# Second MoE under a fixed order of all engines, with an order, banks and places of its own for the first quad

## The chip, the cores and the metric

One core of one Trainium2 chip runs one program: attention, a first MoE and a second MoE, one after the other. The metric is the device time of one execution in microseconds. Engines are named as in the profile: PE (TensorE), DVE (VectorE), ACT (ScalarE), POOL (GpSimd), SP (SyncE, which here only starts DMAs).

## The reference, cut to what matters

The change lies in the last stage. Its input `x` is what attention and the first MoE give, 2304 tokens of 512 values. All of it is computed in float32 (weights arrive as 64-bit floats and are decoded on the chip).

```python
def _moe2_ref(x, w_in, w_out):      # w_in 512 x 2048, w_out 2048 x 512
    h = np.maximum(x @ w_in, 0.0)
    return (h * h @ w_out).astype(np.float32)
```

## The kernel before, in words

The program has two phases. Phase 1 (attention and the first MoE) is written out as a list of tokens, `CFG["phase1"]`, and runs under a manual order of all engines (line 916). Its last products are four `yp` banks; `y_out` (line 614) copies each from PSUM to `ys` on ACT (line 617) and writes it to DRAM with a DMA that ACT starts (line 618).

Phase 2, the second MoE, starts at line 920. There only PE has a manual order: DVE, ACT, POOL and SP are put in order by a list scheduler that works with modelled times, ahead of the run.

**Tiles and quads.** The 2304 tokens are three tiles `t` of 768 (`T2`), and the 2048 columns of `w_in` are eight quads `q` of 256. A tile and a quad make two 2x2 block matrices, multiplied by Strassen's scheme in Winograd's form: seven products P1, P6, P2, P7, P5, P4, P3, in that order (`PRODUCTS`, line 704), each six matmuls of 128x384, since every float32 operand is split into a high and a low half (`mm3`, line 188: high by high, high by low, low by high). The tile's seven operands (A11, A12, A22 and the sums S1 to S4) come from rows `yr` that are read from DRAM (`y_sums`, line 868; sums at line 889), and are split by `y_part` (ACT makes the high half `h...` at line 908, DVE or POOL the low half `l...` at line 910).

**Banks.** `quad` (line 973) has two PSUM banks for the seven products, x and y, which change places from quad to quad. P1 and P2 add up in the first, then P5 and P3 in it; P6, P7 and P4 take turns in the second. So P2 waits for the copy `p` of P1 (ACT, line 994), P7 for u2 (DVE, line 997), P5 for c11 (ACT, line 1000), P4 for u3 (DVE, line 1005), P3 for c22 (DVE, line 1008). The six other banks, `po` (o0 to o5), hold the tile's output and are free in its first quad until `out_group` (line 942) starts them.

**After the products.** Four results c11, c22, c21, c12 are squared (line 1001 for c11, line 982 for the others) and split by `split_g` (ACT `gh`, line 938; DVE `gl`, line 939). From them come twelve output groups of three 128x512 matmuls, two for each of the six `po` banks; they stand between the products of the next quad (line 1018). After a tile's last quad the `po` banks are copied to `ob` (two buffers; the even ones by ACT, line 955, the odd ones by DVE, line 953) and written out by SP (line 957).

**Weights.** Quads 0 to 2 are decoded in phase 1. Quad 3 is decoded by `decode_quad` (line 744), which belongs to phase 2: raw words are loaded (line 167), put together on DVE (lines 172, 181, 184, 739 to 742) and ACT (line 178), and split by `split_cut` (line 727; ACT high half, line 730, POOL low half, line 731). Quads 4 to 7, and all quads of the later tiles, are loaded again from copies in DRAM (`load_quad`, line 858, DMAs at line 864). `spread` (line 1027) puts such steps behind given products.

Of the kernel before, what the change touches and what calls it, by code (L numbers as in the profile page):

```python
# [18 lines left out]
P = 128  # L19
# [98 lines left out]
def local_global_attention__then__moe_kernel(  # L118
# [589 lines left out]
    EARLY = ("A11", "S2", "A12")  # L708
    w2_t = {}
# [34 lines left out]
    def decode_quad(q):  # L744

        raw, tb = {}, {}

        def begin(key, src):
            low, high = raw[key] = raw_words(src, f"{key}_{q}")
            rebias(high)  # L750
            low_bits(low, low)

        def end(key):
            low, high = raw[key]
            join(low, high, low)
# [16 lines left out]
        def last(c, key):  # L772
            end(key)
            split_cut(q, c, raw[key])

        f = 2 * q
        return [
            lambda: begin("f0", wi2[f]),
            lambda: begin("f1", wi2[f + 1]),
            both,  # L780
            other,
            lambda: sums(raw, tb),
            lambda: (split_cut(q, "i1", tb["f0"]), begin("o0", wo2[f]), keep("i0", "i3")),
            lambda: (split_cut(q, "i2", tb["f1"]), begin("o1", wo2[f + 1]), keep("i1", "i2")),
            lambda: last("o0", "o0"),
            lambda: (last("o1", "o1"), keep("o0", "o1")),
        ]
# [132 lines left out]
    with tc.manual_schedule(engines={ENG.PE}):  # L920
# [6 lines left out]

        def product(t, q, ps, a, c, c0, first):
# [6 lines left out]
        def split_g(t, q, name, c):  # L935
            ghi = gp.tile([P, TH], F32R, tag="gh", name=f"gh{t}{q}{name}", bufs=6)
            glo = gp.tile([P, TH], F32R, tag="gl", name=f"gl{t}{q}{name}", bufs=6)
            nc.scalar.activation(out=ghi, in_=c, func=AF.Copy)  # L938
            nc.vector.tensor_tensor(out=glo, in0=c, in1=ghi.bitcast(F32), op=ALU.subtract)  # L939
            return ghi, glo  # L940

        def out_group(t, k, q, i, f, g, last):
# [7 lines left out]
            if last:  # L950
                o = gp.tile([P, DM], F32, tag="ob", name=f"ob{t}_{i}", bufs=2)
                if i % 2:
# [3 lines left out]
                r0 = t * T2 + i * P  # L956
                nc.sync.dma_start(out=out[r0 : r0 + P, :], in_=o)

        def out_groups(t, k, q, g):
# [3 lines left out]
            if k == NQ - 1:  # L963
                order = [(n, i) for i in (0, 1, 2) for n in ("11", "12")] + [(n, i) for i in (3, 4, 5) for n in ("22", "21")]
# [8 lines left out]
        def quad(t, k, q, outs, after):  # L973

            f = lambda tag, name, bufs: gp.tile([P, TH], F32, tag=tag, name=f"{name}{t}{q}", bufs=bufs)
            bank = "xy" if (t * NQ + k) % 2 == 0 else "yx"
            new = lambda j, n: ps_i.tile([P, 512], F32, tag=bank[j], name=f"{n}_{t}{q}")
# [3 lines left out]
            def square(name, c):  # L981
                V.scalar_tensor_tensor(out=c, in0=c, scalar=0.0, in1=c, op0=ALU.max, op1=ALU.mult)  # L982
                g[name] = split_g(t, q, name, c)

            for j, (p, a, c, c0) in enumerate(PRODUCTS):
                if p in ("P2", "P3"):
                    b = ps["P1" if p == "P2" else "P5"]
                else:
                    b = ps[p] = new(p in ("P6", "P7", "P4"), p)
                product(t, q, b, a, c, c0, p not in ("P2", "P3"))  # L990
                d = b[:, 0:TH]
                if p == "P1":
                    got["p1"] = f("p1", "p", 1)
                    A.activation(out=got["p1"], in_=d, func=AF.Copy)
                elif p == "P6":
                    got["u2"] = f("u2", "u2", 1)
                    V.tensor_tensor(out=got["u2"], in0=d, in1=got["p1"], op=ALU.add)  # L997
                elif p == "P2":
                    e = f("c", "c11", 3)
                    A.activation(out=e, in_=d, func=AF.Relu)  # L1000
                    V.tensor_tensor(out=e, in0=e, in1=e, op=ALU.mult)  # L1001
                    g["11"] = split_g(t, q, "11", e)
                elif p == "P7":
                    got["u3"] = f("u3", "u3", 1)
                    V.tensor_tensor(out=got["u3"], in0=d, in1=got["u2"], op=ALU.add)
                elif p == "P5":
                    e = f("c", "c22", 3)
                    V.tensor_tensor(out=e, in0=d, in1=got["u3"], op=ALU.add)
                    square("22", e)
                elif p == "P4":  # L1010
                    e = f("c", "c21", 3)
                    V.tensor_tensor(out=e, in0=got["u3"], in1=d, op=ALU.subtract)
                    square("21", e)
                else:
                    e = f("c", "c12", 3)
                    V.tensor_tensor(out=e, in0=d, in1=got["u2"], op=ALU.add)
                    square("12", e)
# [15 lines left out]
        spread(0, 0, [lambda a=a: y_split(0, a, nc.vector) for a in ("S1", "A22", "S4")], 0)  # L1033
        turns = [list(range(NQ)), [4, 5, 6, 7, 0, 1, 2, 3], list(range(NQ))]
        spread(0, 0, decode_quad(3))
        for t, k in ((t, k) for t in range(NT2) for k in range(NQ - 4)):
            one, two = load_quad(turns[t][k + 4])
            spread(t, k + 1, [one], 1)
            spread(t, k + 2, [two], 1)
        for t in range(NT2 - 1):  # L1040
            spread(t, 5, y_sums(t + 1), 0, 2)
            for j, (_, a, _, _) in enumerate(PRODUCTS):
                spread(t, NQ - 1, [lambda t=t, a=a, j=j: y_split(t + 1, a, nc.gpsimd if j % 2 else nc.vector)], j)
        outs = []
# [53 lines left out]
```

## Time and profile before

| | us |
|---|---|
| three runs, median (lowest to highest) | 826.97 (826.06 to 827.83) |
| the profiled execution, its own time | 826.54 |
| its span, first to last instruction | 824.7 |
| granted TensorE clock, mean | 0.998 |
| PE busy | 807.5 (98%) |
| DVE busy | 522.3 (63%) |
| ACT busy | 321.6 (39%) |
| POOL busy | 184.8 (22%) |

Phase 2 begins on PE at 434.17 us of the span. An engine's idle time is listed with what ended it. Matmuls overlap: the distance between two starts is what a matmul costs, its own length is longer. A busy PE may still run at half its clock, which the distance between starts shows.

### The profile page before, as it was taken

Reading aid. Unit: us, or ns where it says so; the run is one execution under the profiler, and the core shown is the slowest. Engines: PE = TensorE matmul, PEld = TensorE weight load, DVE = VectorE, ACT = ScalarE, POOL = GpSimd, SP = SyncE. Lnnn points to the kernel's source line nnn. Section 1 sums busy time; section 2 is a strip of 40 time slices with the busy share of each in tenths; the row PEclk is TensorE's granted clock in tenths of the full one; section 3 lists DMA queues with packets and bytes.
Section 4 is the critical chain, followed back from the end, with each engine's and each line's share of the span. In section 5 each row is a group of like instructions: output and inputs, shape, how many; then the busy total and the mean of one; then the engine's idle time right before and its main releaser. Section 6 shows DMA issues by size and latency. Waiting matters only on the chain.

```text
span 824.7 us, 15455 instructions
## 1 busy us (share of the span) xinstructions
PE 807.5 (98%) x6130; PEld 748.7 (91%) x6130; DVE 522.3 (63%) x960; ACT 321.6 (39%) x886; POOL 184.8 (22%) x201
## 2 busy tenths in 40 slices
PE   9899999999999999999998999999999999999997
PEld 8789998999999999999997889988898888898886
DVE  5988998797878854326697554467445456444443
ACT  5776555664556523334444121143112133112111
POOL 4665584342025300202544000020000011000000
PEclk9999999999999999999999999999999999999999
DMA  9835437645479500231897653007454003543102
GB/s 279 233 133 198 160 111 242 193 152 175 142 268 309 171 8 8 77 101 39 286 393 257 233 192 113 1 1 230 156 173 130 27 1 117 190 166 117 50 1 77
DMA packets 60624, 121.84 MB, mean 148 GB/s; under 512 B 5288, under 2 KB 29192, under 8 KB 60552
## 3 DMA queue, kind: packets, MB, share of 16 engines
q1 hardware_dynamic: 55944, 116.13, 42.3%
q10 hardware_dynamic: 4608, 4.72, 1.8%
q8 instruction: 48, 0.79, 0.4%
q14 instruction: 24, 0.20, 0.1%
HBM read 88.33 MB, written 32.51 MB: 147 GB/s over the span
## 4 chain that ended last, share of the span: by engine, by line
PE 85%; DVE 7%; DMA 5%; issue 1%; ACT 1%; SPq 0%; POOL 0%; ACTq 0%; DVEq 0%
PE g L189 9%; PE g L191 9%; PE g L190 9%; PE po L190 8%; PE po L189 8%; PE po L191 8%; PE P L189 7%; PE P L191 7%; PE P L190 7%; PE yp L189 3%; PE yp L191 3%; PE yp L190 3%; DMA raw_p<-in_wg 2%; DMA yr<-y 1%; DMA raw_p<-in_wo 1%
## 5 line engine op out<-in xcount | busy, mean ns | idle before, releaser
L189 PE MATMUL g<-xhi,hi_p 128*128 128x256 f32 (+1 forms) x576 | 174.9, 304 | 0.0
L191 PE MATMUL g<-xhi,lo_p 128*128 128x256 f32 (+1 forms) x576 | 170.3, 296 | 0.9 <-DVE lo_p L562 0.9
L190 PE MATMUL g<-xlo,hi_p 128*128 128x256 f32 (+1 forms) x576 | 169.9, 295 | 0.2 <-DVE xlo L517 0.2
L938 ACT ACTIVATE gh<-c 128x384 fp32r<-128x384 f32 x96 | 50.4, 525 | 182.1 <-DVE c L982 163.7
L189 PEld LDWEIGHTS g<-xhi,hi_p 128*128 128x128 f32 x576 | 108.3, 188 | 1.9
L191 PEld LDWEIGHTS g<-xhi,lo_p 128*128 128x128 f32 x576 | 108.2, 188 | 1.3 <-DVE lo_p L562 1.3
L190 PEld LDWEIGHTS g<-xlo,hi_p 128*128 128x128 f32 x576 | 108.7, 189 | 0.4 <-DVE xlo L517 0.4
L939 DVE TENSOR_TENSOR gl<-c,gh 128x384 fp32r<-128x384 f32 x96 | 56.3, 587 | 48.3 <-ACT gh L938 48.2
L591 DVE TENSOR_TENSOR c<-g,c 128x320 f32<-128x320 f32 (+1 forms) x96 | 43.0, 451 | 38.1 <-PE g L191 30.3
L189 PE MATMUL yp<-hh,hi_p 128*128 128x256 f32 (+1 forms) x192 | 58.6, 305 | 0.0
L191 PE MATMUL yp<-hh,lo_p 128*128 128x256 f32 (+1 forms) x192 | 56.8, 296 | 0.0
L190 PE MATMUL yp<-hl,hi_p 128*128 128x256 f32 (+1 forms) x192 | 56.8, 296 | 0.0
L910 POOL TENSOR_TENSOR lS<-s,hS 128x768 fp32r<-128x768 f32 x2 | 3.7, 1841 | 214.8 <-DVE u L997 116.4
L1001 DVE TENSOR_TENSOR c<-c 128x384 f32<-128x384 f32 x24 | 14.3, 597 | 51.4 <-ACT c L1000 51.4
L598 ACT ACTIVATE hh<-c 128x256 fp32r<-128x256 f32 (+1 forms) x48 | 21.0, 441 | 56.5 <-DVE c L591 56.4
L982 DVE SCALAR_TENSOR_TENSOR c<-c 128x384 f32<-128x384 f32 x72 | 41.3, 574 | 2.3
L1000 ACT ACTIVATE c<-P 128x384 f32<-128x384 f32 x24 | 11.8, 492 | 73.9 <-PE P L191 73.9
L323 POOL TENSOR_TENSOR vd<-v 72x128 f32<-72x128 f32 x32 | 21.0, 656 | 81.1 <-PE o30B L473 52.0
L322 POOL TENSOR_TENSOR v<-v 72x256 f32<-72x256 f32 x32 | 26.5, 827 | 47.5 <-DMA v<-in_vP 47.5
L189 PEld LDWEIGHTS yp<-hh,hi_p 128*128 128x128 f32 x192 | 36.3, 189 | 0.6
L190 PEld LDWEIGHTS yp<-hl,hi_p 128*128 128x128 f32 x192 | 36.4, 190 | 0.0
L191 PEld LDWEIGHTS yp<-hh,lo_p 128*128 128x128 f32 x192 | 36.4, 189 | 0.0
(1351 smaller groups left out, 2112.4 us busy)
## 6 DMA issues: line engine op xcount, KB each, us to landing
raw_p<-in_wg SPq DMA_DIRECT2D x9, 1024.0 KB
raw_f<-in_wi SPq DMA_DIRECT2D x7, 1024.0 KB
raw_o<-in_wo SPq DMA_DIRECT2D x7, 1024.0 KB
k<-in_kT SPq DMA_DIRECT2D x16, 291.0 KB
q<-in_qT SPq DMA_DIRECT2D x16, 288.0 KB
v<-in_vP SPq DMA_DIRECT2D x32, 144.0 KB
out_y<-ob SPq DMA_DIRECT2D x18, 256.0 KB
raw_p<-in_wo SPq DMA_DIRECT2D x3, 1024.0 KB
```

Of the source, the lines that this page charges most:

```text
L189: nc.tensor.matmul(ps, whi, xhi, start=first, stop=False, skip_group_check=more)
L190: nc.tensor.matmul(ps, whi, xlo, start=False, stop=False, skip_group_check=more)
L191: nc.tensor.matmul(ps, wlo, xhi, start=False, stop=last, skip_group_check=more)
L322: nc.gpsimd.tensor_tensor(out=v4[:, c, 0:2], in0=v4[:, c, 0:2], in1=v4[:, c, 2:4], op=ALU.add)
L323: nc.gpsimd.tensor_tensor(out=vd[:, c], in0=v4[:, c, 0], in1=v4[:, c, 1], op=ALU.add)
L591: nc.vector.tensor_tensor(out=c_t[b, h, f], in0=ps[:, 0:N], in1=c_t[b, h, f], op=ALU.max)
L598: nc.scalar.activation(out=hhi, in_=c_t[b, h, f], func=AF.Copy)
L938: nc.scalar.activation(out=ghi, in_=c, func=AF.Copy)
L939: nc.vector.tensor_tensor(out=glo, in0=c, in1=ghi.bitcast(F32), op=ALU.subtract)
L982: V.scalar_tensor_tensor(out=c, in0=c, scalar=0.0, in1=c, op0=ALU.max, op1=ALU.mult)
L1000: A.activation(out=e, in_=d, func=AF.Relu)
L1001: V.tensor_tensor(out=e, in0=e, in1=e, op=ALU.mult)
```

## The change

1. Phase 2 puts all five engines under the order in which the code is written. `AFTER` says what follows each product on ACT and DVE; the last split of a quad (h12, l12) comes "late", behind the next quad's first copy. All low halves of tile operands go to DVE.
2. The first quad of the first tile has its own order, `FIRST_QUAD`, and its products P7, P5 and P4 go to the banks o5, o4 and o3 instead of x and y.
3. Quad 3 is decoded in quads 1 to 3, step by step; its raw words are loaded as a step of their own.
4. Places in SBUF: `ys` of the last half batch gets four buffers in another pool and its DMAs start on SP; the first tiles of each tag of phase 2 are set up ahead (`HOMES`, `kept`).
5. The rows of the next tile are asked for in quad 2 of a tile (counted from 0) instead of quad 5, its sums are formed in quads 5 and 6, its operands split in quad 7 and the first quad of the next tile.
6. The output copies of tiles 0 and 1 are all on ACT. The order of the last quad's output groups changes, and the last `ob` is copied and written in two halves, ACT's first, then DVE's.

```diff
     def y_out(b, h, d):
...
+        if (b, h) == (B - 1, 1):
+            ys = yq.tile([P, 320], F32, tag="ys", name=f"ys{b}{h}{d}", bufs=4)[:, 0:N]
+        else:
+            ys = tmp.tile([P, 320], F32, tag="c", name=f"ys{b}{h}{d}")[:, 0:N]
...
-        nc.scalar.dma_start(out=yscr[b][h][:, d, :], in_=ys)
+        (nc.sync if (b, h) == (B - 1, 1) else nc.scalar).dma_start(out=yscr[b][h][:, d, :], in_=ys)
...
+    FRESH = {"P7": "o5", "P5": "o4", "P4": "o3"}
+    late = []
+    AFTER = {
+        "P1": "copy late", "P6": "u2", "P2": "c11 s11 h11", "P7": "u3 l11", "P5": "c22 s22 h22",
+        "P4": "c21 l22 s21 h21", "P3": "c12 s12 l21",
+    }
+    FIRST_QUAD = """
+        HS3 P1 LS3 copy P6 HS1 u2 P2 LS1 HA22 c11 LA22 P7 HS4 P5 u3 P4 LS4 c22 s11 P3 h11 s22 l11 h22 c21 s21 l22 h21
+    """
...
-    with tc.manual_schedule(engines={ENG.PE}):
+    with tc.manual_schedule(engines={ENG.PE, ENG.DVE, ENG.Activation, ENG.Pool, ENG.SP}):
...
+        HOMES = {"ob": (DM, F32, 2), "gl": (TH, F32R, 6), "gh": (TH, F32R, 6), "c": (TH, F32, 3)}
...
+        quad_tiles(3)
+        for tag in HOMES:
+            kept[tag] = home_of(tag, f"{tag}_first")
...
+                if key == (NT2 - 1, 5):
+                    for n, cols in enumerate((slice(0, 256), slice(256, DM))):
+                        if n:
+                            nc.vector.tensor_copy(o[:, cols], po[key][:, cols])
+                        else:
+                            nc.scalar.activation(out=o[:, cols], in_=po[key][:, cols], func=AF.Copy)
+                        (nc.sync if n else nc.scalar).dma_start(out=out[r0 : r0 + P, cols], in_=o[:, cols])
+                    return
+                if i % 2 and t == NT2 - 1:
                     nc.vector.tensor_copy(o, po[key])
                 else:
                     nc.scalar.activation(out=o, in_=po[key], func=AF.Copy)
...
-                order = [(n, i) for i in (0, 1, 2) for n in ("11", "12")] + [(n, i) for i in (3, 4, 5) for n in ("22", "21")]
+                order = order[:4] + order[9:] + order[4:9]
...
+            def new(n):
+                if (t, k) == (0, 0) and n in FRESH:
+                    return ps_o.tile([P, 512], F32, tag=FRESH[n], name=f"{n}_{t}{q}")
+                return ps_i.tile([P, 512], F32, tag=bank[n in ("P6", "P7", "P4")], name=f"{n}_{t}{q}")
...
+            if (t, k) == (0, 0):
+                for token in FIRST_QUAD.split():
+                    run(token)
+                late.extend(lambda x=x: run(x) for x in ("c12", "s12", "l21", "h12", "l12"))
+                return out_groups(t, k, q, g)
+
+            for j, (p, *_) in enumerate(PRODUCTS):
+                multiply(p)
+                for token in AFTER[p].split():
+                    run(token)
                 for call in outs[len(outs) * j // 7 : len(outs) * (j + 1) // 7]:
                     call()
                 for call in after.get(j, ()):
                     call()
+            late.extend((lambda: hi("c12"), lambda: lo("c12")))
...
-        spread(0, 0, decode_quad(3))
+        steps = decode_quad(3)
+        for n, at in enumerate((0, 2, 4, 6, 7, 8, 9, 11, 14, 16)):
+            spread(0, 1, [steps[n]], at)
...
-            spread(t, 5, y_sums(t + 1), 0, 2)
...
+            load, *rest = y_sums(t + 1)
+            spread(t, 2, [load])
+            spread(t, 5, rest, 2, 2)
+            for (_, a, _, _), at in zip(PRODUCTS, (0, 2, 3, 5, 6, 8, 10)):
+                here, at = ((t, NQ - 1), at) if at < 7 else ((t + 1, 0), at - 7)
+                spread(*here, [lambda t=t, a=a: y_split(t + 1, a, nc.vector)], at)
```

In `FIRST_QUAD` a token is a product (P1), a step of `AFTER`, or H and L with an operand: its high half on ACT, its low half on DVE. s squares, h and l split.

What moves, at three places. ACT, from the first operand split of phase 2 on (hS, hA: high halves of operands; p: copy of P1; w3i, w3o: high halves of quad 3's weights; c: c11). Before:

```order
L908 ACTIVATE hS_0_6056<-yr_5274 128x768
L994 ACTIVATE p_6067<-P_00_6060 128x384
L908 ACTIVATE hS_0_6069<-s_0_5278 128x768
L908 ACTIVATE hA_0_6086<-yr_5274 128x768
L908 ACTIVATE hS_0_6106<-s_0_5280 128x768
L730 ACTIVATE w3i_6110<-raw_f_3_6073 128x512
L730 ACTIVATE w3i_6113<-raw_f_3_6073 128x256
L730 ACTIVATE w3i_6111<-raw_f_3_6073 128x512
L730 ACTIVATE w3i_6112<-raw_f_3_6073 128x512
L730 ACTIVATE w3o_6114<-raw_o_3_6167 128x512
L730 ACTIVATE w3o_6115<-raw_o_3_6167 128x512
L1000 ACTIVATE c_6099<-P_00_6060 128x384
```

With the change:

```order
L924 ACTIVATE hS_0_6069<-yr_5274 128x768
L1029 ACTIVATE p_first<-P_00_6071 128x384
L924 ACTIVATE hS_0_6088<-s_0_5278 128x768
L924 ACTIVATE hA_0_6099<-yr_5274 128x768
L1040 ACTIVATE c_first<-P_00_6071 128x384
L924 ACTIVATE hS_0_6111<-s_0_5280 128x768
L1051 ACTIVATE gh_first<-c_first 128x384
L1051 ACTIVATE gh00c_6142<-c_6130 128x384
```

The six splits of quad 3's weights no longer stand ahead of c11.

DVE in the first quad of tile 1 (u: u2 and u3; s, yr: sums of tile 2's operands at line 889; ob: output copies). Before:

```order
L997 TENSOR_TENSOR u_7135<-P_14_7128,p_7123 128x384
L889 TENSOR_TENSOR s_2_7787<-yr_7783 128x768
L1001 TENSOR_TENSOR c_7152<-c_7152 128x384
L953 COPY ob_1_7162<-po_1_6219 128x512
L889 TENSOR_TENSOR yr_7783<-yr_7783 128x2x384
L889 TENSOR_TENSOR s_2_7788<-s_2_7787,yr_7783 128x768
L939 TENSOR_TENSOR gl_7156<-c_7152,gh_7155 128x384
L1005 TENSOR_TENSOR u_7175<-P_14_7168,u_7135 128x384
```

With the change:

```order
L1033 TENSOR_TENSOR u_7128<-P_14_7121,p_7112 128x384
L926 TENSOR_TENSOR lA_1_7138<-yr_6323,hA_1_7136 128x768
L1045 TENSOR_TENSOR c_7146<-c_7146 128x384
L1033 TENSOR_TENSOR u_7166<-P_14_7159,u_7128 128x384
L1057 TENSOR_TENSOR gl14c_7168<-c_7146,gh14c_7149 128x384
L926 TENSOR_TENSOR lS_1_7178<-s_1_6330,hS_1_7176 128x768
```

Tile 2's sums have left this quad (they now stand in the sixth and seventh quad of tile 1); two low halves of tile 1's operands have come in.

PE's last output groups (the first four of twelve; po2_0 is bank o0 of tile 2). Before:

```order
L189 MATMUL po2_0_8307<-w15o0_8722,gh2711_9090 128x512
L190 MATMUL po2_0_8307<-w15o0_8722,gh2711_9090 128x512
L191 MATMUL po2_0_8307<-w15o0_8722,gl2711_9091 128x512
L189 MATMUL po2_0_8307<-w15o1_8723,gh2712_9161 128x512
L190 MATMUL po2_0_8307<-w15o1_8723,gh2712_9161 128x512
L191 MATMUL po2_0_8307<-w15o1_8723,gl2712_9162 128x512
L189 MATMUL po2_1_8320<-w15o0_8722,gh2711_9090 128x512
L190 MATMUL po2_1_8320<-w15o0_8722,gh2711_9090 128x512
L191 MATMUL po2_1_8320<-w15o0_8722,gl2711_9091 128x512
L189 MATMUL po2_1_8320<-w15o1_8723,gh2712_9161 128x512
L190 MATMUL po2_1_8320<-w15o1_8723,gh2712_9161 128x512
L191 MATMUL po2_1_8320<-w15o1_8723,gl2712_9162 128x512
```

With the change:

```order
L189 MATMUL po2_0_8307<-w15o0_8753,gh27c11_9090 128x512
L190 MATMUL po2_0_8307<-w15o0_8753,gh27c11_9090 128x512
L191 MATMUL po2_0_8307<-w15o0_8753,gl27c11_9107 128x512
L189 MATMUL po2_1_8320<-w15o0_8753,gh27c11_9090 128x512
L190 MATMUL po2_1_8320<-w15o0_8753,gh27c11_9090 128x512
L191 MATMUL po2_1_8320<-w15o0_8753,gl27c11_9107 128x512
L189 MATMUL po2_2_8324<-w15o0_8753,gh27c11_9090 128x512
L190 MATMUL po2_2_8324<-w15o0_8753,gh27c11_9090 128x512
L191 MATMUL po2_2_8324<-w15o0_8753,gl27c11_9107 128x512
L189 MATMUL po2_3_8339<-w15o1_8754,gh27c22_9122 128x512
L190 MATMUL po2_3_8339<-w15o1_8754,gh27c22_9122 128x512
L191 MATMUL po2_3_8339<-w15o1_8754,gl27c22_9139 128x512
```

Before, a bank was finished by every second group. Now o0, o1 and o2 are finished by groups 5, 6 and 7, and o3, o4 and o5 by groups 10, 11 and 12.

## Rows read from the trace of the kernel before

**Rows 1.** Windows of 10 us: busy time of each engine, granted clock, DMA share, GB/s

```profile
420.00:430.00 10.00, 10.00 (x76) 10.00 (x75) 8.78 (x15) 5.45 (x11) 3.08 (x3) 1.00 1.04 400
440.00:450.00 10.00, 7.61 (x30) 6.82 (x31) 7.16 (x11) 4.08 (x9) 7.97 (x6) 0.83 0.98 310
```

**Rows 2.** Waits after 420 us: who for whom, total us, times, longest

```profile
PE P L189 <- ACT c L1000: 3.3, 1, 3.3
```

**Rows 3.** Timeline of PE, quads: start us, us, instruction, idle before it

```profile
434.17 0.34 PE L189 MATMUL P<-hA,w0i 128*128 128x384 f32 x1
435.22 0.33 PE L189 MATMUL P<-hS,w0i 128*128 128x384 f32 x1
438.57 0.34 PE L191 MATMUL P<-hS,w0i 128*128 128x384 f32 x1
442.18 0.68 PE L189 MATMUL P<-hS,w0i 128*128 128x384 f32 x1 [3.28 <-ACT c L1000]
...
447.33 0.44 PE L189 MATMUL P<-hA,w1i 128*128 128x384 f32 x1 [0.17 <-DVE c L1012]
...
463.54 0.34 PE L189 MATMUL P<-hA,w2i 128*128 128x384 f32 x1
...
558.15 0.33 PE L189 MATMUL P<-hA,w4i 128*128 128x384 f32 x1
575.41 0.33 PE L189 MATMUL P<-hA,w5i 128*128 128x384 f32 x1
796.25 0.34 PE L189 MATMUL P<-hA,w15i 128*128 128x384 f32 x1
```

**Rows 4.** Timeline of ACT at the start of phase 2

```profile
434.37 0.44 ACT L617 ACTIVATE ys<-yp 128x320 f32<-128x320 f32 x1 [2.20 <-PE yp L191]
...
435.22 0.85 ACT L908 ACTIVATE hS<-yr 128x768 fp32r<-128x768 f32 x1 [0.40 <-ACT ys L617]
435.97 0.47 ACT L994 ACTIVATE p<-P 128x384 f32<-128x384 f32 x1
...
438.54 2.10 ACT L730 ACTIVATE w3i<-raw_f 128x512 fp32r<-128x512 f32 x4
...
441.65 0.48 ACT L1000 ACTIVATE c<-P 128x384 f32<-128x384 f32 x1
```

**Rows 5.** Timelines of DVE and POOL: splits, decoding, a square beside POOL and alone

```profile
432.16 0.69 DVE L184 SCALAR_TENSOR_TENSOR raw_o<-raw_o 128x512 uint32<-128x512 uint32 x1
...
438.30 0.95 DVE L910 TENSOR_TENSOR lA<-yr,hA 128x768 fp32r<-128x768 f32 x1
...
442.16 1.49 DVE L1001 TENSOR_TENSOR c<-c 128x384 f32<-128x384 f32 x1 [1.57 <-ACT c L1000]
...
469.60 0.56 DVE L1001 TENSOR_TENSOR c<-c 128x384 f32<-128x384 f32 x1 [2.42 <-ACT c L1000]
...
439.28 5.53 POOL L731 TENSOR_TENSOR w3i<-raw_f,w3i 128x512 fp32r<-128x512 f32 x4 [14.24 <-ACT w3i L730]
```

**Rows 6.** First quad of tile 1: chain that ended last (the transfer), DVE, PE

```profile
558.92 6.66 DMA yr<-y
...
565.67 0.96 DVE L889 TENSOR_TENSOR s<-yr 128x768 f32<-128x768 f32 x1 [3.84 <-DMA yr<-y]
...
570.42 0.44 PE L189 MATMUL P<-hA,w4i 128*128 128x384 f32 x1 [1.24 <-DVE u L1005]
```

**Rows 7.** The end: timelines of PE, ACT and DVE

```profile
811.97 0.39 PE L189 MATMUL po<-w15o,gh 128*128 128x512 f32 x1
...
820.12 0.39 PE L191 MATMUL po<-w15o,gl 128*128 128x512 f32 x1
...
813.73 0.60 ACT L955 ACTIVATE ob<-po 128x512 f32<-128x512 f32 x1 [1.18 <-PE po L191]
...
817.96 0.69 DVE L953 COPY ob<-po 128x512 f32<-128x512 f32 x1 [2.16 <-DMA out_y<-ob]
821.11 0.69 DVE L953 COPY ob<-po 128x512 f32<-128x512 f32 x1 [2.45 <-DMA out_y<-ob]
```

More of the change, by code (lines that the diff above doesn't have):

```diff
@@ L746, in decode_quad, with load, begin @@
         raw, tb = {}, {}
-        def begin(key, src):
-            low, high = raw[key] = raw_words(src, f"{key}_{q}")
+        def load():
+            for key, src in (("f0", wi2[f]), ("f1", wi2[f + 1]), ("o0", wo2[f]), ("o1", wo2[f + 1])):
+                raw[key] = raw_words(src, f"{key}_{q}")
+        def begin(key):
+            low, high = raw[key]
             rebias(high)
@@ L777, in decode_quad @@
         return [
[L778 to L779 removed]
+            load,
+            lambda: begin("f0"),
+            lambda: begin("f1"),
             both,
@@ new lines, in new, with bank_of, multiply @@
+            def new(n):
+                if (t, k) == (0, 0) and n in FRESH:
+                    return ps_o.tile([P, 512], F32, tag=FRESH[n], name=f"{n}_{t}{q}")
+                return ps_i.tile([P, 512], F32, tag=bank[n in ("P6", "P7", "P4")], name=f"{n}_{t}{q}")
+            def bank_of(p):
+                p = {"P2": "P1", "P3": "P5"}.get(p, p)
+                if p not in ps:
+                    ps[p] = new(p)
+                return ps[p]
+            def multiply(p):
+                _, a, c, c0 = next(x for x in PRODUCTS if x[0] == p)
+                product(t, q, bank_of(p), a, c, c0, p not in ("P2", "P3"))
@@ new lines, in square, with hi, lo @@
+            def square(name):
+                c = got[name]
+                if name == "c11":
+                    V.tensor_tensor(out=c, in0=c, in1=c, op=ALU.mult)
+                else:
+                    V.scalar_tensor_tensor(out=c, in0=c, scalar=0.0, in1=c, op0=ALU.max, op1=ALU.mult)
+            def hi(name):
+                h = home_of("gh", f"gh{t}{q}{name}")
+                A.activation(out=h, in_=got[name], func=AF.Copy)
+                g[name[1:]] = [h]
+            def lo(name):
+                h = g[name[1:]][0]
+                l = home_of("gl", f"gl{t}{q}{name}")
+                V.tensor_tensor(out=l, in0=got[name], in1=h.bitcast(F32), op=ALU.subtract)
+                g[name[1:]].append(l)
@@ new lines, in quad @@
+            STEP = {
+                "copy": copy_p1,
+                "u2": lambda: combine("u2", d("P6"), got["p1"], ALU.add),
+                "c11": lambda: relu("c11"),
+                "u3": lambda: combine("u3", d("P7"), got["u2"], ALU.add),
+                "c22": lambda: combine("c22", d("P5"), got["u3"], ALU.add),
+                "c21": lambda: combine("c21", got["u3"], d("P4"), ALU.subtract),
+                "c12": lambda: combine("c12", d("P3"), got["u2"], ALU.add),
+            }
@@ new lines, in run @@
+            def run(token):
+                kind, rest = token[0], token[1:]
+                if kind == "P":
+                    multiply(token)
+                elif token in STEP:
+                    STEP[token]()
+                elif token == "late":
+                    for call in late:
+                        call()
+                    late.clear()
+                elif kind == "s":
+                    square("c" + rest)
+                elif kind == "h":
+                    hi("c" + rest)
+                elif kind == "l":
+                    lo("c" + rest)
+                elif kind == "H":
+                    y_part(0, rest, "h")
+                else:
+                    y_part(0, rest, "l", nc.gpsimd if kind == "G" else nc.vector)
```

85 lines of the change are left out of this document (28 added, 57 removed).

## The prediction

> **What bounds the kernel now.** I read the windows first. Until the second MoE begins PE is busy all the time (420 to 430 us: 10.00 of 10), and between 440 and 450 only 7.61, with the granted clock at 0.83 [rows 1]. So what ACT, DVE or POOL do before 434 costs nothing, and I look only for stretches in which PE stands still. The waits after 420 us name one large one, 3.3 us for c11 on ACT [rows 2]. PE's timeline gives what each quad really takes [rows 3], and the other timelines say why [rows 4 to 6]. All engines but PE idle much, so their totals say nothing; what counts is who is late at a bank.
>
> The measure is a quad in which nothing is late: from 575.41 to 796.25 us are 14 quads, 15.77 us each [rows 3]. A product is 1.05 us (434.17 to 435.22), seven are 7.35, and the twelve output groups make up the rest, 0.70 each. The first quad has no output groups and could take 7.35 us; it takes 13.16 (434.17 to 447.33) [rows 3]. After P7 (last matmul 438.57) PE waits until 442.18, since P5 goes into c11's bank. c11 starts on ACT at 441.65 only: six splits of quad 3's weights (2.10 us for four of them from 438.54) stand ahead of it in ACT's order [rows 4]. Behind the wait matmuls cost double for a while: the first is 0.68 long instead of 0.34, the lower of the two clock levels, 1.2 instead of 2.4 GHz, which fits the clock of the window [rows 1, 3]. The second quad takes 16.21 (447.33 to 463.54), 0.44 over the measure. The first quad of tile 1 takes 17.26 (558.15 to 575.41), 1.49 over it [rows 3]: DVE stands at tile 2's first sum, for rows that take 6.66 us to arrive, and has u3 behind it, for which P4 waits 1.24 us [rows 6]. The remaining quads show no wait.
>
> **First quad: -5.50 us (from -5.8 to -4.5).** P7, P5 and P4 have banks of their own, so P5 no longer needs c11, nor P7 u2, nor P4 u3. What is late next is the operands' splitting. ACT: the last ys ends at 434.81 [rows 4]; the DMA start between it and the first split is gone, so hS3 runs 434.8 to 435.6, then p (0.47) to 436.0, and at some 0.75 a split (435.22 to 435.97 [rows 4]) hS1 ends at 436.8, hA22 at 437.5, c11 at 438.05 (P2 ends at 437.5), hS4 at 438.8. DVE at 0.95 a low half and about 0.55 for the rest [rows 5], some 0.07 of each overlapped: lS3 to 436.6, u2 437.1, lS1 438.0, lA22 438.9, u3 439.4, lS4 440.3, c22 440.8. PE at 1.05 a product would start P7 at 437.3, P5 at 438.4, P4 at 439.4 and P3 at 440.5; each finds its operands in time but P3, which adds to P5's bank and waits for c22, 0.3 us. The next quad's P1 then starts at 441.85: 7.66 us instead of 13.16. Without that wait it were -5.8; if DVE comes a whole low half (0.95) later, -4.5. With no gap the clock has no reason to fall. o3, o4 and o5 are wanted again only in quad 1 at its third to fifth step, 5 us and more after c21, c12 and u3 have read them.
>
> **Second quad: -0.44 us (from -0.5 to 0).** It goes back to the measure if c21 and c12 are not late for its P1 and P6; x and y are free from c11 and u2 on.
>
> **First quad of tile 1: -1.49 us (from -1.5 to -1.2).** The gain comes from where the sums stand on DVE, not from reading sooner: before, the scheduler had put both the reads and the sums into the first quads of the tile, back to back. Now three quads (47 us) lie between a read and its first sum, against 6.66 us for the transfer [rows 6]. The price, two low halves of DVE (0.95 each) in that quad and five in the quad before, lies beside 15.77 us of PE and about 7 us of other DVE work (13 operations of 0.55); I cost it at nothing. If that cover were gone it would be at most two of 0.95 for u3. All six output copies of a tile on ACT (0.60 each [rows 7]) also lie beside PE.
>
> **Decoding of quad 3: 0 (to +1.1).** The same instructions, now in quads 1 to 3, where the steady work leaves DVE half idle. The tightest place is u2 of quad 2. Counted from that quad's start: the first two joins (0.69 each [rows 5]) end at 1.8, ACT's high half at 2.45, POOL's low half (5.53/4 = 1.38 [rows 5]) at 3.85; if DVE's l12 is held until then, the next two joins end at 5.8 and u2 at 6.35, and P7 wants it at 3 x 1.05 + 5 x 0.70 = 6.65. So 0.3 us are spare; with one more POOL operation in the way u2 is 1.1 late.
>
> How much POOL holds DVE decides this. c11's square took 1.49 us beside POOL's low halves and 0.56 alone [rows 5], so 0.93 was lost once. The Trainium skill (SBUF: State Buffer, "Who interferes with whom") has it that a VectorE operation with two SBUF inputs and a GpSimd operation that reads SBUF exclude each other, the later one waiting until the other ends. By that rule each of the six POOL operations may hold one DVE operation for its whole length, which would be the first rival below. The trace agrees in kind: 0.93 is less than one POOL operation.
>
> **The end: +1.2 us (from +0.3 to +2.1).** This speaks against the change. Groups go at 0.70 us (811.97 to 820.12 for 35 steps [rows 7]) and a bank can be copied some 0.15 after its last group. Before, one bank was finished every 1.4 us; a buffer is free again 2.16 to 2.45 us after its copy, and the last copy ended at 821.80 [rows 7]. Now o0, o1, o2 are finished by groups 5, 6, 7 and o3, o4, o5 by 10, 11, 12, with the same two buffers. ob0 runs 815.7 to 816.3, ob1 816.4 to 817.05; ob3 wants ob1's buffer: from 819.2 or 819.5, ends at 819.9 to 820.2; ob5 wants ob3's: from 822.1 to 822.6. Its halves have one tile, and DVE's write of it follows ACT's: about 0.38 (0.44 for 320 columns [rows 4]) and 0.42, so the last copy ends at 822.9 to 823.5, 1.1 to 1.7 later than before. The last transfer has half the bytes, for which I take off 0.2: +1.2. The lower end has halves of exactly half length and 0.6 off the transfer, the upper one no shorter than wholes. The Trainium skill (DMA: Bandwidth & Descriptors, the table of cost components) gives a transfer 2.0 us fixed and the bytes by 436 GB/s beside; by that half a block would save 0.3 us, an estimate, and the sum would be 0.1 lower. No run here shows it.
>
> **Sum.** -5.50 - 0.44 - 1.49 + 1.2 = -6.2 us. On the profiled execution (826.54; 824.7 of it span) that is 820.3. The median shown, 826.97, is 0.43 above that execution: 820.7 is the forecast. With all bounds: -7.5 to -2.5, the decoding's 1.1 among them, but not all ends meet; I use 819.0 to 822.5 as the forecast's own range.
>
> **Rivals.**
> - *The decoding becomes the wait* (quads 1 to 3). For: the 0.3 us of room, the 0.93 lost above. Against: u2 alone is tight, and reads PSUM. One to three misses of 1.1 us: 821.8 to 824.0.
> - *DVE takes ACT's place in the first quad.* Seven of its operations stand in a row ahead of c22 with no gap. If operand splits run as slowly as the square did (0.93 more for three of them), PE idles, the clock falls and doubled matmuls follow: half of the 5.5 us returns, 823.5.
> - *No change.* The first quad's wait reappears in full behind o3 to o5 or c22; then -1.9 + 1.2 remain: about 826.2.
> - *Slower: output copies block ACT at tile changes.* ACT has six copies in a row with two buffers, and the next quad's p behind them. With 2.2 us from copy to free buffer ob3 (its bank done at 13.3 us of the tile, ACT still at two splits) ends at 14.8, ob5 at 17.6, and P2 of the next quad wants p by 15.75 + 4.2: after p itself (0.5) some 1.8 us are spare. It decides from 4.6 us on, where ob5 waits for ob3's write and this for ob1's: each further us costs 2 us at two tile changes. At 6.7 us it costs 8.4, and the sum is 829.2. The only transfer here that took so long carried six times the bytes (a tile's rows, 1.57 MB against 0.26) [rows 6]; against it stand 2.16 and 2.45 [rows 7].
>
> **How the numbers follow.** Forecast 0.74; decoding 0.12; DVE in the first quad 0.06; no change 0.04; slower 0.03; better than 819.0, 0.01. About 0.2% (1.65 us) can be told from no change. Faster is what ends below 825.3: 0.74 + 0.12 + 0.06 + 0.01 = 0.93; same 0.04; slower 0.03. The range 818.9 to 823.3 holds the forecast's own range with the spread of runs and the nearer half of the first rival.
>
> **What would show it.** Right: P5 of the first quad starts right behind P7, quad 1's P1 near 441.9; the granted clock is 1.00 in every window from 440 on; no wait of 1 us for u3 at the first quad of tile 1; the last ob copies wait for a DMA, with DVE's half ending about 2.5 us or more after PE's last matmul (1.3 before). Wrong: PE waits above 0.5 us in quads 1 to 3 for u2 or c22, or waits for p in a tile's second quad; or a tail no longer than before.

## The result, and the profile after

The changed kernel takes 819.66 us (median of 4 runs, 818.96 to 821.19), the kernel before, run beside it, 827.09 (826.06 to 827.83). The ratio is 0.9914, with a 95% interval of 0.9896 to 0.9931: faster by 7.4 us, where 6.3 were predicted. The profiled run takes 818.96 us, 817.2 of it span; before it was 826.54 and 824.7.

PE's timeline of the changed kernel answers to [rows 3] (columns as there). The rows are P1 of quads 0, 1 and 2, of the first two quads of tile 1 and of the last quad; P4's last and P3's first matmul in the first quad; the last matmul of all.

```profile
433.23 0.34 PE L189 MATMUL P<-hA,w0i 128*128 128x384 f32 x1
...
439.36 0.34 PE L191 MATMUL P<-hA,w0i 128*128 128x384 f32 x1
439.81 0.41 PE L189 MATMUL P<-hS,w0i 128*128 128x384 f32 x1
...
440.94 0.34 PE L189 MATMUL P<-hA,w1i 128*128 128x384 f32 x1
...
456.75 0.34 PE L189 MATMUL P<-hA,w2i 128*128 128x384 f32 x1
...
551.36 0.33 PE L189 MATMUL P<-hA,w4i 128*128 128x384 f32 x1
...
567.10 0.33 PE L189 MATMUL P<-hA,w5i 128*128 128x384 f32 x1
...
787.93 0.34 PE L189 MATMUL P<-hA,w15i 128*128 128x384 f32 x1
...
811.64 0.39 PE L191 MATMUL po<-w15o,gl27c 128*128 128x512 f32 x1
```

These rows and those of before, subtracted, split the 7.5 us of span without a remainder. The third column is the changed kernel profiled once more (x0, below).

| stretch on PE, us | before | changed | again | difference (changed) |
|---|---|---|---|---|
| start of the second MoE | 434.17 | 433.23 | 433.97 | -0.94 |
| first quad, P1 to the next P1 | 13.16 | 7.71 | 7.72 | -5.45 |
| second quad | 16.21 | 15.81 | 15.80 | -0.40 |
| first quad of tile 1 | 17.26 | 15.74 | 15.73 | -1.52 |
| the other 20 quads up to the last | 315.45 | 315.44 | 315.46 | -0.01 |
| last quad's P1 to PE's last matmul | 24.26 | 24.10 | 24.09 | -0.16 |
| from there to the end of the span | 4.19 | 5.17 | 5.13 | +0.98 |

The windows (columns as in [rows 1]) show a PE that is full at 1.00 of the clock from the first quad on, where before 7.61 of 10 us were busy at 0.83:

```profile
430.00:440.00 10.00, 9.89 (x61) 9.59 (x60) 5.37 (x8) 4.68 (x8) 0.00 (x0) 1.00 0.54 197
440.00:450.00 10.00, 10.00 (x52) 9.18 (x52) 7.09 (x15) 4.00 (x8) 0.00 (x0) 1.00 0.95 314
```

On ACT c11 now starts 5.10 us earlier than in [rows 4] (4.16 counted from P1); on DVE its square takes 0.55 us instead of the 1.49 of [rows 5]:

```profile
436.55 0.49 ACT L1040 ACTIVATE c_first<-P 128x384 f32<-128x384 f32 x1
```

```profile
439.11 0.55 DVE L1033 TENSOR_TENSOR c<-P,u_first 128x384 f32<-128x384 f32 x1
439.58 0.55 DVE L1045 TENSOR_TENSOR c_first<-c_first 128x384 f32<-128x384 f32 x1
```

Tile 2's rows are issued on SP at 571.27, 19.9 us behind the tile's first product (551.36), and DVE's first sum over them runs 65 us later, with no transfer named as what it waits for, unlike [rows 6]:

```profile
571.27 2.10 SPq L896 DMA_DIRECT2D yr<-y  x3
```

```profile
636.68 0.95 DVE L905 TENSOR_TENSOR s<-yr 128x768 f32<-128x768 f32 x1
```

In the code the rows are now asked for three quads sooner, but in time they are read later: in the kernel before SP issued them at 557.67, half a microsecond ahead of the tile's first product (558.15).

```profile
557.67 1.89 SPq L880 DMA_DIRECT2D yr<-y  x3
```

The end, ACT and then DVE, answers to [rows 7]. From the third copy on each is released by the transfer that empties the place two copies back, and DVE's half by ACT's half; the last copy ends at 814.55, 2.52 us after PE (1.29 before).

```profile
807.30 0.60 ACT L988 ACTIVATE ob<-po 128x512 f32<-128x512 f32 x1 [3.07 <-PE po L191]
810.07 0.60 ACT L988 ACTIVATE ob<-po 128x512 f32<-128x512 f32 x1 [2.17 <-DMA out_y<-ob]
812.86 0.60 ACT L988 ACTIVATE ob<-po 128x512 f32<-128x512 f32 x1 [2.19 <-DMA out_y<-ob]
813.71 0.38 ACT L982 ACTIVATE ob<-po 128x256 f32<-128x256 f32 x1 [0.26 <-DMA out_y<-ob]
```

```profile
814.13 0.42 DVE L980 COPY ob<-po 128x256 f32<-128x256 f32 x1 [2.58 <-ACT ob L982]
```

### The profile page after: what moved, and what is told of

The parts are those of the page before. It is cut to its first block, busy times and chain, and to the rows that moved or that the text cites. A ratio compares the mean times of both kernels' runs of the same rounds, so it can differ in the third digit from the quotient of the medians.

```text
span 817.2 us, 15421 instructions
## 1 busy us (share of the span) xinstructions
PE 805.1 (99%) x6130; PEld 748.2 (92%) x6130; DVE 514.3 (63%) x960; ACT 321.3 (39%) x893; POOL 173.7 (21%) x195
## 4 chain that ended last, share of the span: by engine, by line
PE 90%; DVE 6%; DMA 2%; ACT 0%; issue 0%; SPq 0%; ACTq 0%; DVEq 0%
PE g L189 10%; PE g L191 9%; PE g L190 9%; PE po L190 8%; PE po L189 8%; PE po L191 8%; PE P L189 7%; PE P L191 7%; PE P L190 7%; PE yp L189 3%; PE yp L190 3%; PE yp L191 3%; DMA raw_p<-in_wg 1%; DVE raw_p L546 1%; DMA v<-in_vP 1%; DMA out_y<-ob 0%
## 5 line engine op out<-in xcount | busy, mean ns | idle before, releaser
L1033 DVE TENSOR_TENSOR c<-P,u 128x384 f32<-128x384 f32 x46 | 25.6, 556 | 32.4 <-PE P L191 32.4
L322 POOL TENSOR_TENSOR v<-v 72x256 f32<-72x256 f32 x32 | 29.3, 915 | 43.7 <-DMA v<-in_vP 43.7
L323 POOL TENSOR_TENSOR vd<-v 72x128 f32<-72x128 f32 x32 | 18.0, 561 | 80.6 <-PE o30B L473 52.0
L546 DVE SCALAR_TENSOR_TENSOR raw_p<-raw_p 128x1024 uint32<-128x1024 uint32 x24 | 34.0, 1428 | 0.0
L1029 ACT ACTIVATE p<-P 128x384 f32<-128x384 f32 x23 | 11.3, 490 | 51.4 <-PE P L191 51.4
```

Of the source, the lines that this page charges most:

```text
L322: nc.gpsimd.tensor_tensor(out=v4[:, c, 0:2], in0=v4[:, c, 0:2], in1=v4[:, c, 2:4], op=ALU.add)
L323: nc.gpsimd.tensor_tensor(out=vd[:, c], in0=v4[:, c, 0], in1=v4[:, c, 1], op=ALU.add)
L546: nc.vector.scalar_tensor_tensor(out=low, in0=high, scalar=scalar, in1=in1, op0=op0, op1=ALU.bitwise_or)
L1029: A.activation(out=got["p1"], in_=ps["P1"][:, 0:TH], func=AF.Copy)
L1033: V.tensor_tensor(out=got[out], in0=p, in1=b, op=op)
```

## The experiments

My theory, after the result: the first quad had two causes in one place, c11 late in ACT's queue and products waiting for c11's bank, so that either remedy alone gives nearly all; at tile 1 it is where the sums stand; at the end, copies that wait for places. The rivals are that one remedy alone carries the first quad, that reading sooner carries tile 1, and that the end is lost elsewhere. Each edit is shown against the changed kernel. The readings go by stretches of PE's timeline: where an edit does not touch a stretch it repeats within 0.02 us, while whole times do not (x0).

### x0: the same kernel again

> The changed kernel once more, unedited. The median lies near 819.7 us. The second MoE begins on PE at 433.2 us in the changed kernel's profile and at 434.2 in the profile of before, although the order around the place where the 0.94 us arise is the same in both. If that is a difference between executions (my theory), this run's start may lie anywhere from 433 to 434.5 us, and the stretches behind it repeat within 0.1 us: first quad 7.7 us, second 15.8, first of tile 1 15.7, last quad's start to the end 29.3. If the change moved something in phase 1 (rival), the start is again at 433.2.

Measured: 820.99 us (8 runs, 819.73 to 823.62), ratio 0.9936 (0.9909 to 0.9962). The second MoE starts at 433.97; first quad 7.72, second 15.80, first of tile 1 15.73, last quad to the end 29.22. So the stretches repeat and the start does not: over the nine profiles of kernels whose first phase is the same it lies between 432.12 (x4) and 438.12 (x7). The 434.17 of before lies inside that spread, so nothing shows the 0.94 us at the start to be the change's.

### x1: the first quad with two banks

```diff
-    FRESH = {"P7": "o5", "P5": "o4", "P4": "o3"}
+    FRESH = {}
```

> The first quad's last three products go back into the two banks x and y, its order and the place of quad 3's decoding stay those of the change. My theory: freeing ACT's queue ahead of c11 carries nearly all of the first quad; without the banks of their own the next quad's P1 waits in y for c21, so the first quad lasts about 8.6 us (8.3 to 9.0) instead of 7.72, first and second quad together 24.4 instead of 23.5. Rival (the banks carry the gain, since c11 and c22 must empty x and y before PE goes on): 12 to 13 us.

Measured: first quad 8.57, the first two 24.47 (23.52 in the changed kernel). PE's one wait in it is for c21, as forecast:

```profile
443.03 0.44 PE L189 MATMUL P<-hA,w1i 128*128 128x384 f32 x1 [0.70 <-DVE c L1033]
```

Moving the decoding alone (ACT's queue free ahead of c11, POOL idle), without the banks, is 0.95 us from the whole. The rival is out.

### x2 and x3: quad 3's decoding ahead again, with and without the banks

```diff
-  ... HS1 u2 P2 LS1 HA22 c11 LA22 P7 HS4 P5 u3 ...
+  ... HS1 u2 P2 LS1 HA22 HS4 W c11 LA22 P7 P5 u3 ...
+            if token == "gA315":
+                d3["load"]()
+                d3["begin"]("f0")
...
+                elif kind == "W":
+                    d3["cuts"]()
...
-        for n, at in enumerate((0, 2, 4, 6, 7, 8, 9, 11, 14, 16)):
-            spread(0, 1, [steps[n]], at)
+        spread(0, 1, [lambda: d3["keep"](*CUT)], 0)
```

x3 has `FRESH = {}` as well. `W` stands for the six `split_cut` of quad 3, each a high half on ACT and a low half on POOL.

> Quad 3's decoding goes back to the end of phase 1 and its six splits on ACT ahead of c11, as before; the banks of the change stay. My theory: with banks of their own P7, P5 and P4 no longer need c11 done, so ACT's delay of about 3.3 us falls on no product; only POOL's low halves beside DVE delay c22 and P3: first quad 8 to 9 us, first and second quad together 1 to 3 us over the change's 23.5. Rival (ACT's queue ahead of c11 is all of it, banks or not): the first quad 12 us or more.

> Both back: the splits on ACT ahead of c11, and two banks. My theory: PE again waits about 3.3 us for c11 and then runs for a while at the lower of its two clocks; first quad 12.5 to 13.5 us (13.16 before). If it stays under 11 us, it is the first quad's own order of instructions, which stays that of the change here, that carries part of the gain (rival).

Measured in x3: first quad 14.06, second 15.93. PE's waits there:

```profile
442.43 0.54 PE L189 MATMUL P<-hS,w0i 128*128 128x384 f32 x1 [3.13 <-ACT c_first L1064]
449.01 0.44 PE L189 MATMUL P<-hA,w1i 128*128 128x384 f32 x1 [1.60 <-DVE c L1057]
```

The wait for c11 is back (3.28 before) and the clock falls to 0.66 of full in the five us behind it; a second wait, 1.60 for c21, which stands on DVE behind a square of 1.66 us beside POOL, makes it longer than before and than I expected. The new order of instructions by itself saves nothing.

Measured in x2: first quad 8.46, as expected, but the second 19.68: together 28.14, 4.62 over the change where I expected 1 to 3. PE never waits for c11. It waits for DVE; below PE's two waits, then DVE, then POOL.

```profile
440.25 0.41 PE L189 MATMUL P<-hS,w0i 128*128 128x384 f32 x1 [0.86 <-DVE c L1057]
445.12 0.50 PE L191 MATMUL po<-w0o,gl_first 128*128 128x512 f32 x1 [1.85 <-DVE gl_first L1081]
```

```profile
437.95 1.68 DVE L934 TENSOR_TENSOR lS<-s,hS 128x768 fp32r<-128x768 f32 x1
439.55 0.55 DVE L1057 TENSOR_TENSOR c<-P,u_first 128x384 f32<-128x384 f32 x1
...
441.84 1.66 DVE L1071 SCALAR_TENSOR_TENSOR c<-c 128x384 f32<-128x384 f32 x1
443.42 1.64 DVE L1081 TENSOR_TENSOR gl_first<-c_first,gh_first 128x384 fp32r<-128x384 f32 x1
```

```profile
437.50 5.58 POOL L743 TENSOR_TENSOR w3i<-raw_f,w3i 128x512 fp32r<-128x512 f32 x4 [13.78 <-ACT w3i L742]
```

Beside POOL the low half took 1.68 us instead of 0.95, and a square and the next low half 1.66 and 1.64 instead of 0.55. The operation at 439.55, which has one of its two inputs in PSUM, took its usual 0.55. So in x2 two things were late together: c11, through ACT, and DVE, through POOL. The next two runs take them apart.

### x9 and x12: the low halves elsewhere

```diff
-                    d3["cuts"]()
+                    for call in d3["cuts"]("h"):
+                        call()
...
-        spread(0, 1, [lambda: d3["keep"](*CUT)], 0)
+        spread(0, 1, d3["cuts"]("l"), 2, 2)
+        spread(0, 1, [lambda: d3["keep"](*CUT)], 13)
```

These lines are against x2; x12 also replaces `nc.gpsimd` by `nc.vector` in the separate low halves.

> As x2 (banks of their own, quad 3's words put together in phase 1, its six high halves on ACT ahead of c11), but POOL's six low halves stand in the second and third quad instead of beside c11's square. My theory: what x2 lost, 4.6 us over the change's 23.5 for the first two quads, came from POOL and DVE holding each other up (c22, s11, l11 each took about 1.6 us instead of 0.55), not from c11 starting 3.3 us later on ACT; without POOL there the two quads last 23.5 to 24.3 us. Rival (c11's delay on ACT is what reaches l11 and PE): 26 us or more.

> As x9, but the six low halves of quad 3 are made by DVE itself, spread over the second and third quad, so POOL does nothing in phase 2 (in x9 POOL's queue had no wait in it and ran the six at 438.5 as in x2). The six high halves stay on ACT ahead of c11, which so starts about 7 us after P1 instead of 3.3. My theory: POOL and DVE holding each other up is what x2 and x9 lost; without POOL l4 takes 0.95 us again, c22 is not late, s11 and l11 end about 9.2 us after P1 and PE wants l11 at 9.6: first quad 7.7 to 7.9 us, first and second together 23.5 to 24.0. Rival (c11's lateness on ACT is what reaches l11 and PE): the wait for gl_first stays, over 1 us, and the two quads last 25 us or more.

x9 missed: 8.46 and 18.15, together 26.61. It did not do what it was made for. POOL's queue holds nothing else there, so its six operations ran as soon as their high halves were there, at the same place as in x2, whatever stood between them in the program; PE's two waits are 0.86 and 1.85 again. What differs is the clock: these one-us windows begin 0.9 us behind the second wait, of x2 first, then of x9.

```profile
446.00:447.00 1.00, 1.00 (x5) 1.00 (x4) 1.00 (x2) 0.32 (x1) 0.23 (x1) 0.50 1.06 412
```

```profile
447.00:448.00 1.00, 1.00 (x7) 0.91 (x7) 1.00 (x2) 0.32 (x1) 0.23 (x1) 1.00 0.99 346
```

In x2 the clock was at its lower level, 1.2 GHz, from half a microsecond behind the wait until about 449; in x9 it stayed at 2.4 after waits of the same length. The next twelve matmuls take 4.00 us in x2 (445.45 to 449.45) and 2.47 in x9 (446.45 to 448.92): that is the 1.53 us between the two kernels.

x12 settles it: 7.73 and 15.93, together 23.66 (23.5 to 24.0 expected), and no wait on PE above 0.13. c11 starts 6.96 us after P1, as late as in x9, but DVE has its old durations, in the same places:

```profile
441.41 0.95 DVE L938 TENSOR_TENSOR lS<-s,hS 128x768 fp32r<-128x768 f32 x1
...
443.87 0.56 DVE L1073 TENSOR_TENSOR c_first<-c_first 128x384 f32<-128x384 f32 x1 [1.05 <-ACT c_first L1068]
...
445.03 0.56 DVE L1085 TENSOR_TENSOR gl_first<-c_first,gh_first 128x384 fp32r<-128x384 f32 x1
```

So with banks of their own a c11 that is 3.6 us late costs 0.14 us, and POOL beside DVE cost the rest of x9 and x2, with the clock's fall in x2. The first two quads in all cases, in us:

| kernel | own banks | ACT free ahead of c11 | POOL idle beside DVE | first two quads |
|---|---|---|---|---|
| before | no | no | no | 29.37 |
| x3 | no | no | no | 29.99 |
| x2, x9 | yes | no | no | 28.14, 26.61 |
| x12 | yes | no | yes | 23.66 |
| x1 | no | yes | yes | 24.47 |
| changed | yes | yes | yes | 23.52 |

No run has POOL idle, no banks of their own and a full ACT queue. PE would have x3's wait of 3.13 for c11 there too, since POOL doesn't delay c11: it starts 6.96 or 6.97 us after P1 in x2, x3, x9 and x12 alike. That is argued and was not tried.

### x4 and x5: the rows of the next tile

```diff
-            spread(t, 2, [load])
-            spread(t, 5, rest, 2, 2)
+            if t == 1:
+                spread(t, 1, [load, *rest[:2]], 1, 0)
+                spread(t, 1, rest[2:], 2, 0)
+            else:
+                spread(t, 2, [load])
+                spread(t, 5, rest, 2, 2)
```

x5 only replaces `spread(t, 2, [load])` by `spread(t, 5, [load])`.

> Tile 2's rows are read in the second quad of tile 1 and summed on DVE at once, right behind the read, ahead of that quad's u3; all else as in the change. My theory: the gain at the tile's start came from where the sums stand on DVE, behind rows that have long landed, not from the time of reading itself. So here DVE stands until the rows have landed, PE waits for u3 as it did before in the first quad of tile 1, and that quad lasts 1.5 to 3.5 us longer than 15.8; the quads behind it stay at 15.7 to 15.8. Rival (the order on DVE doesn't matter, the rows come early enough): every quad 15.7 to 15.8.

> The rows are read at the sixth quad of a tile, as the code before had it, and summed two to eight products later, as in the change. The read of tile 1 then stands behind the loads of w7, about 504.5 us by the change's profile, and lands 7 to 9 us after; the first sum stands at 510.5. My theory: the place of the sums carries the gain, a late read only makes DVE wait 1 to 3 us in a quad in which it is half idle: PE waits 0 to 1 us in each of two quads, all other quads 15.7 to 15.8. Rival (reading three quads sooner carries it): PE waits 1.2 us or more each time, and the clock falls behind it. Rival the other way: no wait at all.

x4: the second quad of tile 1 takes 23.13 us instead of 15.79, the others are unchanged; the wait is 5.17 for u3, and the clock falls to its lower level in it, at about 579.6, and stays there until about 586.4. The kind is right, the size (1.5 to 3.5) far too small: I had not counted that SP's read stands behind the tile's six output copies (issued at 568.11, 2.1 us into the quad), nor that the transfer needs 7.9 us beside the weights' loads. SP, DVE, PE, and the granted clock in the window around the wait's end:

```profile
568.11 1.91 SPq L896 DMA_DIRECT2D yr<-y  x3
```

```profile
577.39 0.96 DVE L905 TENSOR_TENSOR s<-yr 128x768 f32<-128x768 f32 x1 [7.86 <-DMA yr<-y]
```

```profile
582.20 0.69 PE L189 MATMUL P<-hA,w5i 128*128 128x384 f32 x1 [5.17 <-DVE u L1033]
```

```profile
580.00:585.00 5.00, 2.80 (x8) 2.71 (x9) 4.08 (x8) 0.90 (x2) 0.00 (x0) 0.50 0.47 184
```

x5: every quad as in the changed kernel (15.72 to 15.82), no wait; I expected up to 1 us twice. SP had the read out at 491.86 (and the other tile's at 617.57), not at 504.5, and the sums came 19 us later:

```profile
491.86 5.45 SPq L896 DMA_DIRECT2D yr<-y  x4
```

```profile
511.06 0.95 DVE L905 TENSOR_TENSOR s<-yr 128x768 f32<-128x768 f32 x1
```

So reading three quads sooner is worth nothing here, and sums right behind their read make PE wait. That their new place is worth all of the 1.52 us is not shown: before, one of DVE's output copies, which the change moved to ACT, stood between the first sum and u3 as well.

```profile
567.01 0.68 DVE L953 COPY ob<-po 128x512 f32<-128x512 f32 x1
```

The next operation starts 0.60 us after it, so some 0.6 of the wait of 1.24 us would have gone with the copy alone (an estimate). No run has the copies on DVE and the sums in their new place, or the reverse in the tile's first quad.

### x6, x7, x8 and x10: the end

```diff
+                if t == NT2 - 1:
+                    order = [(n, i) for i in (0, 1, 2) for n in ("11", "12")] + [(n, i) for i in (3, 4, 5) for n in ("22", "21")]
```

```diff
-        HOMES = {"ob": (DM, F32, 2), ...
+        HOMES = {"ob": (DM, F32, 3), ...
```

```diff
+                    o2 = home_of("c", f"ob{t}_{i}b")
...
+                    nc.vector.tensor_copy(o2[:, 0:256], po[key][:, 256:DM])
+                    nc.sync.dma_start(out=out[r0 : r0 + P, 256:DM], in_=o2[:, 0:256])
```

x6 is the first edit, x7 the second, x8 the second and third, x10 the first and second with the last tile copied whole by ACT.

> The last tile's six output groups in the order of before (11 and 12 interleaved, then 22 and 21), two places. My theory: the order by slots made the last group's copy wait for a place, so the way from the last quad's start to the end returns from 29.3 us to 28.5 as before. Rival (the order of the groups doesn't matter, the 0.8 us are the cover lost with the shorter quads): 29.3.

> Three places for output tiles, nothing else. My theory: the last copies no longer wait for places, only the second half for the first: 27.6 us from the last quad's start to the end instead of 29.3. Rival (the shared tile of the halves alone is what costs): 29.3 stays.

> Three places for output tiles instead of two, and the last tile's two halves in a tile each. My theory of the end: the last copies wait for places (2.2 to 2.45 us from a copy's end to the place free again) and the second half waits for the first because both write one tile. Then the way from the last quad's start to the end falls from 29.3 us to 27.2 (26.8 to 27.6), about 2 us off the whole. Rival (the fixed time from the last output's issue to its landing decides and the places are hidden): 29.0 or more.

> The last tile's groups in the order of before (pairs of one bank in a row), three places for output tiles, and the last tile copied whole by ACT (0.60 us) instead of in two halves one behind the other (0.38 and 0.42). My theory: no copy waits for a place or for another copy, the last one ends some 0.7 us after PE's last matmul (1.1 in x6, 0.9 in x8, 2.5 in the change), and from the last quad's start to the end it is 27.6 us (27.3 to 27.9) against 29.2 in the change and 28.0 in x6 and x8: the shortest of all. Rival (what is left is the last transfer's own time, longer for 256 KB than for 128): 28.0 or more.

| kernel | last quad's P1 to PE's end | PE's end to last copy's end | last copy's end to span's end | sum |
|---|---|---|---|---|
| before | 24.26 | 1.29 | 2.90 | 28.45 |
| changed | 24.10 | 2.52 | 2.65 | 29.27 |
| x6 | 24.31 | 1.11 | 2.59 | 28.01 |
| x7 | 24.09 | 0.92 | 3.06 | 28.07 |
| x8 | 24.10 | 0.92 | 2.96 | 27.98 |
| x10 | 24.31 | 0.68 | 3.19 | 28.18 |

All four win 1.1 to 1.3 us; in the nine profiles whose end no edit touches (the changed kernel, x0 to x5, x9, x12) the sum is 29.16 to 29.64. So the lost time was the waits for places, and the old order (x6) or a third place (x7) takes them off the end; in x6 the last block still waits for one, but only until 0.28 us after PE's last matmul. x6 came out better than the 28.5 expected. x7, x8 and x10 missed (27.6, 27.2 and 27.6 expected): none gets below about 28.0. With a third place the last copy ends sooner, but the stretch behind it is 2.96 to 3.19, against 2.65 in the changed kernel and 2.59 in x6. Why is open, and 0.4 us of that stretch can differ between executions by themselves (the last section). x10's 28.18 is on its rival's side, but that the whole block is the reason is not shown: the stretch is 2.90 before, with a whole block, and 3.06 in x7, with halves. In x8 the halves run one behind the other although each has a tile of its own (ACT, then DVE):

```profile
811.40 0.38 ACT L979 ACTIVATE ob<-po 128x256 f32<-128x256 f32 x1
```

```profile
811.82 0.42 DVE L981 COPY ob_5b<-po 128x256 f32<-128x256 f32 x1 [1.08 <-ACT ob L979]
```

The program makes DVE wait for ACT there, and what they still share is the bank of po. The Trainium skill (PSUM: Partial Sum Buffer, "Terms") has it that two engines on one bank at once are an error, reads against reads included. The trace agrees in that the two follow each other, 811.40 and 811.82; no run here has them side by side. x8 gains nothing from the second tile: from PE's end its copies lie as in x7. That the bank is the reason is argued from the page; it was not tried.

Whole times: x8 819.79 us, ratio 0.9913 (0.9879 to 0.9947), x10 819.45, ratio 0.9907 (0.9885 to 0.9928), the changed kernel on x8's chip 0.9936 (0.9909 to 0.9962). The intervals overlap; that x6 and x8 are 1.2 us better than the change is shown by the stretch and not by the total.

## Why the prediction was right

- **First quad**, -5.50 forecast, -5.45 measured. P5 no longer waits, P3 starts 0.27 us late for c22 (439.81 instead of 439.54; 0.3 forecast), quad 1's P1 comes 7.71 us after quad 0's (7.66 forecast), the clock stays up. x1, x3 and x12 show that the two parts of the change are alternatives, where POOL does not work beside DVE: with banks of their own and POOL there (x2, x9) the first two quads keep only 1.2 and 2.8 of the 5.85 us.
- **Second quad**, -0.44 and -0.40; **first quad of tile 1**, -1.49 and -1.52. The step "from where the sums stand on DVE, not from reading sooner" holds by x4 and x5, but for the output copy's share, which is open. Between a read and its first sum lie 65 and 69 us where I counted 47, since SP asks for the rows ahead of their place in the code.
- **Decoding of quad 3**, 0 and 0. The tight place had more room than I gave it: u2 of quad 2 ends 6.03 us into the quad (6.35 forecast, 6.65 wanted).
- **The end**, +1.2 forecast, +0.82 measured. The last copy ends 2.52 us after PE, inside the 2.4 to 3.0. That the halves follow each other was right; that they do so for the one tile was not, for in x8 they follow each other with a tile each. What was mis-sized is small: PE's own part of the last quad is 0.16 shorter (not in my sum), and the last transfer 0.25 shorter (0.2 taken off).
- **The sum**, -6.2, against -6.55 in the stretches that I summed. The other 0.94 of the 7.5 us lie before the second MoE, where nothing shows them to be the change's. That the whole came out 7.4 us here is thus in part luck; next to x0 the medians differ by 5.3 (826.26 and 820.99).

The rivals: decoding did not become the wait, though its mechanism is there. In the changed kernel POOL's low halves, then DVE beside them:

```profile
466.47 1.31 POOL L743 TENSOR_TENSOR w3i<-raw_f,w3i 128x512 fp32r<-128x512 f32 x1 [2.75 <-ACT w3i L742]
469.40 1.69 POOL L743 TENSOR_TENSOR w3i<-raw_f,w3i 128x512 fp32r<-128x512 f32 x1 [1.62 <-ACT w3i L742]
```

```profile
462.23 0.55 DVE L1033 TENSOR_TENSOR u<-P,p 128x384 f32<-128x384 f32 x1
...
466.46 0.55 DVE L1033 TENSOR_TENSOR c<-P,u 128x384 f32<-128x384 f32 x1
467.04 1.16 DVE L1047 SCALAR_TENSOR_TENSOR c<-c 128x384 f32<-128x384 f32 x1
...
469.37 0.55 DVE L1057 TENSOR_TENSOR gl02c<-c,gh02c 128x384 fp32r<-128x384 f32 x1
469.84 1.66 DVE L1047 SCALAR_TENSOR_TENSOR c<-c 128x384 f32<-128x384 f32 x1
```

The square begun at 469.84 ends at 471.50, 0.41 us after POOL (471.09), the one at 467.04 again 0.42 after POOL (467.78); the operation at 466.46, with one input in PSUM, is not held. It goes the other way too: DVE's low half at 469.37, with both inputs in SBUF, began before POOL's at 469.40, which then took 1.69 instead of 1.31. The Trainium skill's rule (SBUF: State Buffer, "Who interferes with whom"), that a VectorE operation with two SBUF inputs and a GpSimd operation that reads SBUF exclude each other, agrees with these rows. In quads 1 to 3 there is slack for it; in x2 and x9, where PE follows DVE closely, it cost 4.5 and 3.0 us against x12. Rival two had priced 2.8 for three DVE operations held so. The slower rival, copies that block ACT at the tile's change, needed a place that is free again 4.6 us or more after its copy; it takes 2.17 and 2.19 at the end, and PE has no wait in a second quad of a tile.

## What to carry to other kernels

When a wait has two causes in series, a late producer and a shared bank, either cure can give nearly all of the gain (x1, x12), so don't add the two up; but look at what else comes with each, as POOL did with the banks alone (x2). Put a sum behind its read by more than the transfer's time in the queue of the waiting engine; 19 us between them (x5) did as well here as 65. Before moving POOL work that reads SBUF beside a DVE chain that TensorE follows closely, count each DVE operation with two SBUF inputs as lasting until 0.4 us after POOL's ends (469.84 above). And a place in the program does not delay an engine whose queue is empty: POOL's six operations ran as early in x9 as in x2.

## What was not expected of the hardware

- After the same two waits of PE (0.86 and 1.85 us) the granted clock fell to 0.50 for some 3.4 us in x2 and not at all in x9: 1.53 us. Waits of 0.70 (x1), 1.24 (tile 1 before) and 1.60 (x3) left it at full level; 3.13 (x3), 3.28 (before) and 5.17 (x4) did not.
- The last quad takes PE 24.26 to 24.31 us where the two groups of a bank follow each other (before, x6, x10), and 24.09 to 24.10 in the other order, with no gap in either.
- The stretch from the last copy to the end of the span is 3.02 us in x5 and 2.55 to 2.65 in the eight other profiles that end alike: 0.4 us at the very end can come without a cause in the kernel.
